# A gated long-convolution and MLP kernel with its filter transform folded twice, shift transfers on GpSimd, more norm applies on ScalarE and reordered output pairs

## The chip, the cores and the metric

The kernel runs on one core of one Trainium2 chip, in one launch. The metric is the device time of that core in microseconds, from the start of the program to its end; less is better. The arithmetic is in bf16, with sums in float32.

## The reference

The input x is 2048 rows of 640 columns. Two branches work on it and a gate mixes them.

```
g = sigmoid((x * gate_w).sum(-1))
# branch a: a causal convolution as long as the sequence
kv = (sum over 4 taps of shifted k * shift_k) * v
y  = irfft(rfft(kv padded to 4096) * rfft(ssm_k padded to 4096))[:2048] + kv * ssm_D
a  = x * y
# branch b: token shift and MLP
h  = gelu(layernorm(x) @ w1)                  # 640 -> 640
hs = the four quarters of h's columns, shifted by +1, -1, +2, -2 rows, @ w2
x1 = x + hs
b  = x1 + gelu(layernorm(x1) @ w3) @ w4       # 640 -> 1536 -> 640
out = g * a + (1 - g) * b
```

## The kernel before

The rows are 16 tiles of 128, in four blocks of 512. One SBUF arena holds everything, and its regions are used again and again by later stages.

**First norm and first layer.** `ln1` takes the mean and variance of each tile on VectorE (`bn_stats`), the power -0.5 on GpSimd, and applies both to the tile. For tiles 0 to 7 the result is transposed on TensorE and evicted by ScalarE; for tiles 8 to 15 VectorE applies the norm (`ln_apply`) and a DMA transposes it. `mm1` multiplies by w1, five groups of 128 features, with a gelu on ScalarE behind each. The fifth group holds the last 32 features of each quarter, which are to be shifted by different numbers of rows: line 924 copies four strips of 32 partitions from the gelu's buffer `hx` into `hT`, each at its own offset, on VectorE. The other four groups need no copy, since `mm2` reads them at an offset.

**Second layer and second norm.** `mm2(t)` multiplies the shifted features by w2 and adds x (on TensorE by an identity for tiles 0 to 7, in line 959 on VectorE for the rest). `ln2` takes the row sums that come with it. `ln_math` is three steps on GpSimd and, between the second and the fourth, one on VectorE: the variance, a one-column tensor_scalar. For tiles 0 to 7 VectorE applies the norm, for 8 to 15 ScalarE; a DMA transposes. `mm3` and `mm4` are the layers of the MLP, in blocks of 512 rows.

**The filter.** ssm_k is transformed once, in five chunks of 128 channels. `h_load` brings a chunk in; `h_fold` makes even and odd parts of it about its middle (`krev` is the reversed copy that ScalarE makes, `fo` the two parts, 1024 columns each), and two DMA transposes turn them into `het`. `h_chunk` multiplies them by cosine and sine tables (`Rh`, and `Zn` for two special rows), 20 matmuls of 512 columns a chunk, and ScalarE evicts the spectrum to `HF`.

**The convolution.** For two halves of 320 channels (g) and four blocks of 512 rows (b), `kv_block` forms kv and folds it, `x_fwd` transforms it, `combine` prepares the sums between blocks. `unit(hh, c)` multiplies spectra on VectorE, 2560 columns at a time. Some of its sums are made by accumulating DMAs from GpSimd's queue.

**The output.** `final(hh, c, q, k)` transforms back one pair of tiles: TensorE, an eviction on ScalarE, a sum and a difference on VectorE, a flip on TensorE, a scaled eviction on ScalarE, the product with q on VectorE. The k-th of the 16 pairs is added to the output by an accumulating DMA from GpSimd where k is below `KACC` = 12; for the last four, VectorE adds the MLP's part from `X`, and SyncE stores plainly. Where a pair accumulates, `base(t)` has stored a first value of that row's MLP branch (the scaled residual) and `mm4(t)` has accumulated its product; where it doesn't, an identity matmul in `mm4` brings the residual in.

**The order.** Each engine runs its instructions in order. The order is a list of operation numbers written out by hand, `SEQUENCE`; `schedule` walks it with a cost model that only chooses PSUM banks and a few extra dependencies. SyncE issues the plain loads and stores and all transposes, GpSimd the accumulating DMAs. Line 669 is the helper of tensor_tensor, 674 of tensor_scalar, 679 of ScalarE's activations, 689 of matmuls, 861 of the power on GpSimd, 237 of a DMA's issue and 234 of a transpose's.

Of the kernel before, what the change touches and what calls it, by code (L numbers as in the profile page):

```python
# [7 lines left out]
U16 = mybir.dt.uint16  # L8
# [4 lines left out]
class Op:  # L13
    __slots__ = ("idx", "eng", "fns", "ins", "outs", "dur", "bias", "nbytes", "preds", "succs", "rank",
                 "tp", "early", "cost", "free", "grp", "tile", "ordinal", "waits", "inc", "value", "dsem", "dval", "snap", "snapd", "start", "end", "order", "lat")

    def __init__(self, idx, eng, fns, ins, outs, dur, bias, nbytes):
        self.idx = idx
        self.eng = eng
        self.fns = fns  # L20
        self.ins = ins
        self.outs = outs
        self.dur = dur
        self.bias = bias
        self.nbytes = nbytes
        self.preds = {}
        self.succs = []
# [5 lines left out]
        self.lat = 0.0  # L33
        self.free = None
        self.tile = None
# [87 lines left out]
def regions(ap):  # L123
# [3 lines left out]
    t = ap.tensor  # L127
# [26 lines left out]
    for lo, hi in runs:  # L154
        b0, b1 = (f0 + lo) * esz, (f0 + hi) * esz
# [18 lines left out]
class Prog:  # L174
# [51 lines left out]
    def dma(self, queue, out, in_, bias=0.0, transpose=False, slow=False, free=None, early=False, accum=False, fn=None):  # L226
# [11 lines left out]
        issue = (350.0 + n / 90.0) if transpose else (970.0 if queue == "pool" else 470.0)  # L238
# [5 lines left out]
        op.cost = n * esz / 256 * 1.65 if transpose else n * esz / run * ((46 + 0.087 * run) if accum else (8 + 0.0435 * run)) / 16  # L244
# [26 lines left out]
    def schedule(self, sequence, backlog=3000.0):  # L271
# [4 lines left out]
        done = []  # L276
        avail = [0.0] * 8
# [4 lines left out]
        for i in sequence:  # L282
            o = ops[i]
            st = max([free[o.eng]] + [ops[p].end + d for p, d in delays[i]])
            if o.nbytes and not o.tp and not o.early:
                st = max(st, dfree - backlog)
            t = o.tile
# [15 lines left out]
            if o.nbytes:  # L303
                dfree = max(st + 0.5 * o.dur, dfree) + o.cost
                o.end = max(dfree, o.end) + o.lat
                if o.cost > 500 and not o.tp and not o.early:
# [122 lines left out]
def _folded_dft():  # L429
# [12 lines left out]
    p = np.arange(128)[:, None]  # L442
    no = np.stack([p, p + 128])
    ne = np.where(no == 0, 256, no)
    Rh = np.stack([np.cos(w * 2 * k * ne),
                   np.where(k == 0, no == 0, -np.sin(w * 2 * k * no)),
                   np.cos(w * (2 * ko + 1) * no),
                   -np.sin(w * (2 * ko + 1) * ne)])
    Z = np.zeros((3, 128, 128))
    Z[:2, :, 0] = ((-1.) ** ne)[:, :, 0]  # L450
    Z[2, 0] = 1.
# [6 lines left out]
    Rh = Rh.transpose(2, 0, 1, 3)  # L458
    G = G.reshape(2, 2, 2, 128, 256).transpose(3, 0, 2, 1, 4)
    return (R, np.concatenate([Rh.reshape(128, 2048), Z.transpose(1, 0, 2).reshape(128, 384)], 1),  # L460
            G.reshape(128, 8 * 256))


def bass_gated_mix__ssm_conv_h3__mixer_s_mlp__prompt_kernel(
# [33 lines left out]
    def ps(n, cls):  # L498
# [3 lines left out]
    SEQUENCE = [2, 3, 10, 11, 12, 31, 6, 57, 8, 1, 13, 14, 15, 16, 17, 18, 19, 20, 21, 22, 23, 24, 25, 7, 9, 0, 4, 28, 5, 56, 29, 63, 58, 64,  # L502
# [684 lines left out]
```

## Time and profile before

| | |
|---|---|
| Median of 3 runs | 235.55 us (234.9 to 235.9) |
| The profiled execution | 235.56 us, span 233.8 us |
| TensorE (PE) busy | 221.1 us, 95% |
| VectorE (DVE) busy | 220.1 us, 94% |
| ScalarE (ACT) busy | 170.3 us, 73% |
| GpSimd (POOL) busy | 105.9 us, 45% |
| DMA | 45.48 MB, mean 195 GB/s |

The span runs from the first to the last instruction on the core; the rest of the execution's time lies around it. Busy time is the time in which an engine has at least one instruction under way. A row of the groups names a line, an engine, an operation, its shapes and its count, then the busy time, the mean time of one, and the idle time of the engine just before such instructions, with what ended it.

### The profile page before, as it was taken

The page shows a single profiled execution, that of the slowest core. Times are in us where ns is not written, and L with a number is a line of the kernel's source. Part 1 is how long each engine was busy: PE and PEld are TensorE (multiplying, and loading weights), DVE is VectorE, ACT ScalarE, POOL GpSimd, SP SyncE. Part 2 cuts the span into 40 slices and gives each one's busy share as a digit, 9 for nine tenths or more (in the row PEclk, how much of TensorE's full clock was granted, in tenths as well). Part 3 has the DMA queues.
Part 4 walks back from the last instruction along what each step waited for, and adds up shares of the span by engine and source line. Part 5 has one row for each costly group of instructions (what it writes and reads, how often), then busy time and mean ns, then how long its engine had stood idle before and what let it go on. Part 6 is the DMA issues. An engine that isn't in the chain of part 4 may idle for free.

```text
span 233.8 us, 4171 instructions
## 1 busy us (share of the span) xinstructions
PE 221.1 (95%) x1501; PEld 134.6 (58%) x1501; DVE 220.1 (94%) x402; ACT 170.3 (73%) x317; POOL 105.9 (45%) x122
## 2 busy tenths in 40 slices
PE   7999999989998999999999999999999999999960
PEld 2598665436554656544775456654666556776630
DVE  6998999999988999998999999999989999979994
ACT  2799699488796899769949897577655387288881
POOL 0330406274495801196376693246024332456870
PEclk9999999999999999999999999999999999999997
DMA  5999959898878999978638988999978987989998
GB/s 161 360 345 250 253 146 271 246 277 204 140 181 176 240 213 317 343 212 180 157 97 145 187 189 163 146 191 206 259 142 145 196 140 142 185 98 111 95 109 165
DMA packets 63785, 45.48 MB, mean 195 GB/s; under 512 B 28818, under 2 KB 59028, under 8 KB 63764
## 3 DMA queue, kind: packets, MB, share of 16 engines
q1 hardware_dynamic: 54748, 33.33, 55.2%
q0 software_dynamic: 8832, 11.80, 34.9%
q8 instruction: 12, 0.20, 0.3%
q10 hardware_dynamic: 184, 0.08, 0.1%
q14 instruction: 9, 0.07, 0.1%
HBM read 24.22 MB, written 6.55 MB: 132 GB/s over the span
## 4 chain that ended last, share of the span: by engine, by line
PE 45%; DVE 9%; POOL 3%; ACT 2%; issue 1%
PE PSall L689 45%; DVE arena L669 8%; ACT arena L679 2%; POOL arena L674 1%; POOL arena L861 1%; POOL arena L669 1%; DVE arena L959 0%; DVE arena L674 0%
## 5 line engine op out<-in xcount | busy, mean ns | idle before, releaser
L689 PE MATMUL PSall<-arena 128*128 128x320 bf16 (+5 forms) x1444 | 213.7, 307 | 5.3 <-DVE arena L669 2.4
L669 DVE TENSOR_TENSOR arena<-arena 128x640 bf16<-128x640 bf16 (+5 forms) x247 | 182.3, 793 | 3.0 <-ACT arena L679 1.9
L689 PEld LDWEIGHTS PSall<-arena 128*128 128x128 bf16 (+1 forms) x1444 | 130.5, 98 | 86.9 <-DVE arena L669 4.2
L679 ACT ACTIVATE arena<-PSall 128x512 bf16<-128x512 f32 (+6 forms) x189 | 107.7, 634 | 29.4 <-PE PSall L689 25.2
L679 ACT ACTIVATE arena<-arena 128x640 bf16<-128x640 bf16 (+4 forms) x62 | 42.2, 703 | 6.7 <-POOL arena L669 2.7
L861 POOL TENSOR_TENSOR arena<-arena 128x1 f32<-128x1 f32 (+1 forms) x26 | 29.3, 1128 | 31.9 <-DVE arena L674 31.5
L674 POOL TENSOR_SCALAR arena<-arena 128x1 f32<-128x1 f32 (+2 forms) x41 | 24.8, 608 | 34.7 <-DVE arena L959 12.0
L237 POOL DMA_DIRECT2D out_dram<-arena x28 | 30.5, 1197 | 20.5 <-ACT arena L679 15.0
L679 ACT ACTIVATE arena<-PSall,arena 128x640 bf16<-128x640 f32 (+1 forms) x32 | 20.6, 658 | 20.0 <-PE PSall L689 19.9
L237 POOL DMA_DIRECT2D arena<-arena x12 | 14.9, 1242 | 32.1 <-DVE arena L669 28.2
L674 DVE TENSOR_SCALAR arena<-arena 128x640 bf16<-128x640 bf16 (+2 forms) x49 | 14.4, 307 | 3.4 <-POOL arena L674 1.6
L857 DVE BATCH_NORM_STATS2 arena<-arena 128x6 f32<-128x320 bf16 x32 | 14.6, 479 | 2.0 <-DMA arena<-in_A_q_dram 1.7
L669 POOL TENSOR_TENSOR arena<-arena 128x1 f32<-128x1 f32 (+1 forms) x11 | 10.3, 943 | 2.9 <-DVE arena L674 2.5
L715 PE MATMUL PSall<-arena 128*128 128x512 bf16 x15 | 5.4, 536 | 1.6 <-DVE arena L711 1.6
L959 DVE SCALAR_TENSOR_TENSOR arena<-PSall,arena 128x640 bf16<-128x640 f32 x8 | 6.4, 808 | 0.1
L924 DVE TENSOR_SCALAR arena<-arena 32x256 bf16<-32x256 bf16 (+1 forms) x24 | 5.9, 244 | 0.5
L679 ACT ACTIVATE PSall<-PSall 128x640 f32<-128x640 f32 x8 | 5.6, 699 | 0.1
L715 PEld LDWEIGHTS PSall<-arena 128*128 128x128 bf16 x15 | 1.9, 132 | 4.6 <-issue 2.5
L903 PE MATMUL PSall<-arena 128*128 128x128 bf16 x40 | 3.6, 219 | 0.3
L718 ACT ACT_TABLE_LOAD x1 | 1.3, 1283 | 2.7 <-issue 2.7
L903 PEld LDWEIGHTS PSall<-arena 128*128 128x128 bf16 x40 | 2.4, 97 | 1.4 <-DVE arena L858 0.4
L858 DVE BATCH_NORM_AGGREGATE arena<-arena 128x2 f32<-128x12 f32 x16 | 3.0, 197 | 0.0
(24 smaller groups left out, 9.6 us busy)
## 6 DMA issues: line engine op xcount, KB each, us to landing
arena<-arena POOLq DMA_DIRECT2D x12, 640.0 KB, 6.3
arena<-in_A_k_dram SPq DMA_DIRECT2D x14, 400.0 KB, 4.1
arena<-in_A_q_dram SPq DMA_DIRECT2D x14, 320.0 KB, 6.9
out_dram<-arena POOLq DMA_DIRECT2D x20, 160.0 KB, 4.2
arena<-in_A_ssm_k_dram SPq DMA_DIRECT2D x5, 512.0 KB, 4.4
arena<-in_A_v_dram SPq DMA_DIRECT2D x16, 160.0 KB, 3.9
arena<-in_B_w_dram SPq DMA_DIRECT2D x1, 1920.0 KB, 8.8
out_dram<-arena SPq DMA_DIRECT2D x10, 160.0 KB, 3.7
```

The costliest lines, as they stand in the source:

```text
L237: fn = lambda e: e.dma_start(out, in_, **kw)
L669: P.op(eng, lambda e: e.tensor_tensor(o, real(a), real(b), op), [a, b], [o], dve_ns(o, [a, b], 2) if eng == "dve" else 500)
L674: P.op(eng, lambda e: e.tensor_scalar(o, real(a), s1, s2, op0=op0, **({} if op1 is None else {"op1": op1})), [a] + aps, [o], dve_ns(o, [a] ...
L679: P.op("act", lambda e: e.activation(real(o), real(a), f, bias=bias, scale=scale, **({"accum_out": accum} if accum is not None else {})), ...
L689: fns.append(lambda e, l=l, r=r, i=i: e.matmul(real(o), l, r, start=(i == 0), stop=(i == last)))
L715: P.op("pe", lambda e: e.matmul(real(pw), warm[:, 0:128], warm[:, 128:640], start=True, stop=True), [warm], [pw], 427.0 if i < 14 else 216.0)
L857: P.op("dve", lambda e, o=o, i=i: e.bn_stats(o, i), [i], [o], 400)
L858: P.op("dve", lambda e: e.bn_aggr(bna[:, t, :], bns[k]), [bns[k]], [bna[:, t, :]], 120)
L861: P.op("pool", lambda g: g.tensor_tensor(o, a, e, ALU.pow), [a, e], [o], dur)
L903: P.op("pe", [lambda e, c=c, pb=pb, xn=xn: e.transpose(real(pb)[:, 128 * c:128 * (c + 1)], xn[:, 128 * c:128 * (c + 1)], ident) for c in r ...
L924: P.op("dve", lambda e, o=hT[q, 4, c0:c0 + n], i=hx[q, :]: e.tensor_scalar(o, i, 1.0, None, op0=ALU.mult), [hx[q, :]], [hT[q, 4, c0:c0 + n ...
L959: P.op("dve", lambda e: e.scalar_tensor_tensor(x, real(pr), 1.0, x, op0=ALU.mult, op1=ALU.add, accum_out=st[1, 0][:, t:t + 1]), [pr, x], [ ...
```

## The change

- **The filter's even bins are folded twice.** `h_fold` now takes the reversed copy in halves, and puts the element at the middle into two places, with five small steps in place of two. `h_chunk` first forms the sum and the difference of the two halves of `het` on VectorE (two operations of 1024 columns, `pq`), and repairs one partition of them (two of 512). The even bins then take one matmul where they took two; a chunk has 15 matmuls of 512 columns in place of 20. `pq` lies where the chunk's loaded filter lay, so the load of the chunk after next waits for these matmuls. The table `Rh` shrinks from 2432 to 1920 columns.
- **Shift transfers on GpSimd.** For blocks 1 to 3 the four strips are moved by DMAs from GpSimd's queue, 16 in all; block 0 keeps VectorE's copies.
- **More norm applies on ScalarE.** For tiles 8 to 15 of the first norm GpSimd computes minus mean times rstd, and ScalarE applies the norm.
- **The variance step** of the second norm goes from VectorE to GpSimd, for all 16 tiles.
- **Output pairs.** The pairs of blocks 2, 1, 0 of both halves come first (k from 0 to 11), and those of block 3 of both halves last. So tiles 12 to 15 are stored plainly, and their `base` and accumulating stores are gone; tiles 0 to 7 now have a `base` of 640 columns where it was 320.
- **The order list** is written anew for all engines. In GpSimd's queue the shift transfers stand among the steps of both norms. On VectorE the four new steps of filter chunks 0 and 1 stand between the kv products of half 0, and those of chunks 2 to 4 later, around the last products of half 0 and the first of half 1. The first output pairs stand ahead of most of half 1's spectral products.
- Some of the planner's durations differ, it now limits the descriptors in flight on SyncE, and accesses count as whole 4-byte words.

The diff, cut to its core:

```diff
@@ regions
-        b0, b1 = (f0 + lo) * esz, (f0 + hi) * esz
+        b0, b1 = (f0 + lo) * esz // 4 * 4, ((f0 + hi) * esz + 3) // 4 * 4
@@ schedule
+            while o.ring and sum(r for e, r in ring if e > st) + o.ring > 2048:
+                st = min(e for e, r in ring if e > st)
...
-    SEQUENCE = [2, 3, 10, 11, 12, 31, 6, 57, 8, 1, 13, 14, 15, 16, 17, 18, 19, 20, 21, 22, 23, 24, 25, 7, 9, 0, 4, 28, 5, 56, 29, 63, 58, 64,
...
+    hpq = [V(oXF + 10240 + 2048 * i, 2048).rearrange("p (e s b c) -> p e s b c", e=2, s=2, b=4) for i in range(2)]
@@ h_fold
-        act(kr[:, :, 1:256], k[:, :, 511:256:-1], ACTF.Copy)
-        tt(fo[:, 1], k[:, :, 0:256], kr, ALU.subtract)
-        tt(fo[:, 0], k[:, :, 0:256], kr, ALU.add)
-        ts(fo[:, 0, :, 0:1], k[:, :, 256:257], 1.0, None, ALU.mult)
+        back = bass.AP(AR, k.offset + 511, [list(k.ap)[0], [512, 4], [-256, 2], [-1, 127]])
+        act(kr[:, :, :, 1:128], back, ACTF.Copy)
+        halves = k.rearrange("p b (h n) -> p b h n", h=2)[:, :, :, 0:128]
+        f4 = fo.rearrange("p e b (h n) -> p e b h n", h=2)
+        tt(f4[:, 1], halves, kr, ALU.subtract)
+        tt(f4[:, 0], halves, kr, ALU.add)
+        tt(f4[:, 0, :, 0, 0:1], k[:, :, 128:129], k[:, :, 384:385], ALU.add)
+        tt(f4[:, 1, :, 1, 0:1], k[:, :, 128:129], k[:, :, 384:385], ALU.subtract)
+        tt(f4[:, 1, :, 1, 0:1], f4[:, 1, :, 1, 0:1], k[:, :, 0:1], ALU.add)
@@ h_chunk
+        tt(pq[:, :, 0], ev[:, :, :, 0, :], ev[:, :, :, 1, :], ALU.add)
+        tt(pq[:, :, 1], ev[:, :, :, 0, :], ev[:, :, :, 1, :], ALU.subtract)
+        for s, op in ((0, ALU.add), (1, ALU.subtract)):
+            tt(pq[0:1, 0, s], ev[0:1, 1, :, 0, :], ev[0:1, 0, :, 1, :], op)
...
-                pairs = [(Rh[:, y, kk, 128 * m:128 * (m + 1)], ev[:, eo, :, kk, :]) for kk in range(2)]
-                if y == 0:
-                    pairs.append((Zn[:, 2, :], ev[:, 1, :, 0, :]))
-                if j == 0 and r == 1:
-                    pairs += [(Zn[:, kk, :], ev[:, 0, :, kk, :]) for kk in range(2)]
+                if j < 2:
+                    pairs = [(Rhe[:, r, m, :], pq[:, r, m])]
+                else:
+                    pairs = [(Rho[:, r, kk, 128 * m:128 * (m + 1)], ev[:, 1 - r, :, kk, :]) for kk in range(2)]
+                if j == 0:
+                    pairs += [(Zn[:, 0, :], ev[:, 0, :, 0, :])] if r == 0 else [(Zn[:, 1, :], pq[:, 0, 0]), (Zn[:, 2, :], ev[:, 0, :, 0, :])]
@@ ln_math
-        ts(s[3], s[1], s[4], None, ALU.subtract)
+        tt(s[3], s[1], s[4], ALU.subtract, eng="pool")
@@ ln1
+            if t >= LN1A:
+                rstd, off = st[0, 5][:, t:t + 1], st[0, 4][:, t:t + 1]
+                ts(off, bna[:, t, 0:1], -1.0, rstd, ALU.mult, ALU.mult, eng="pool")
+                act(xn, x, ACTF.Identity, scale=rstd, bias=off)
+                P.dma(sp, xt[:, :, (t % 4) * 128:(t % 4 + 1) * 128], xn, transpose=True)
+                continue
@@ mm1
+                    if sc >= 1:
+                        P.dma("pool", hT[q, 4, c0:c0 + n], hx[q, :])
+                        continue
@@ summed, tile_rows, base, mm4
-        return 8 * hh + 2 * (3 - t // 4) < KACC
+        return t < 12
...
+        if t >= 12:
+            return
...
+        if t < 12:
+            x, o = tile_rows(t)
+            P.dma("pool", o, x, accum=True)
@@ the pairs
-    for hh in range(2):
-        for c in (3, 2, 1, 0):
-            for q in range(2):
-                at(final, hh, c, q, 8 * hh + 2 * (3 - c) + q)
+    k = 0
+    for group in ((2, 1, 0), (3,)):
+        for hh in range(2):
+            for c in group:
+                for q in range(2):
+                    at(final, hh, c, q, k)
+                    k += 1
```

More of the change, by code (lines that the diff above doesn't have):

```diff
@@ L14 @@
     __slots__ = ("idx", "eng", "fns", "ins", "outs", "dur", "bias", "nbytes", "preds", "succs", "rank",
-                 "tp", "early", "cost", "free", "grp", "tile", "ordinal", "waits", "inc", "value", "dsem", "dval", "snap", "snapd", "start", "end", "order", "lat")
+                 "tp", "early", "cost", "free", "grp", "tile", "ordinal", "waits", "inc", "value", "dsem", "dval", "snap", "snapd", "start", "end", "order", "lat", "ring")
     def __init__(self, idx, eng, fns, ins, outs, dur, bias, nbytes):
@@ L237, in dma @@
             fn = lambda e: e.dma_start(out, in_, **kw)
-        issue = (350.0 + n / 90.0) if transpose else (970.0 if queue == "pool" else 470.0)
+        issue = (1240.0 + n / 1200.0) if transpose else 970.0 if queue == "pool" else 530.0
         op = Op(len(self.ops), queue, [fn], [in_], [out], issue, bias, n * esz)
@@ L243, in dma @@
         run = esz * min(run_of(out), run_of(in_))
-        op.cost = n * esz / 256 * 1.65 if transpose else n * esz / run * ((46 + 0.087 * run) if accum else (8 + 0.0435 * run)) / 16
+        op.cost = n * esz / 256 * 1.72 if transpose else n * esz / run * ((46 + 0.087 * run) if accum else (8.4 + 0.0457 * run)) / 16
+        op.ring = 0 if queue == "pool" else n * esz // 256 if transpose else n * esz // run
+        if queue != "pool" and op.ring > 200 and not transpose:
+            op.dur = 660.0
         op.lat = 1150.0 if transpose else 3000.0 if accum else 2300.0
@@ L441, in _folded_dft @@
                         -np.sin(w * (2 * ko + 1) * n), -np.sin(w * (2 * ko + 1) * m)], 1)
[L442 to L451, printed above, removed]
+    i = np.arange(128)[:, None]
+    th, ph = w * 2 * k * i, lambda a: w * (2 * ko + 1) * a
+    cos, sin, row = np.cos(th), -np.sin(th), i == 0
+    sin[0] = np.sin(np.pi / 2 * k)[0]
+    sin[:, 0:128] *= ~row
+    b0 = np.cos(ph(128))
+    Rh = np.concatenate([cos[:, 0:128], cos[:, 128:256], sin[:, 0:128], sin[:, 128:256],
+                         np.where(row, 1 - b0, np.cos(ph(i))), np.where(row, b0, -np.cos(ph(256 - i))),
+                         -np.sin(ph(np.where(row, 128, i))), -np.sin(ph(256 - i)),
+                         np.where(row, np.cos(np.pi / 2 * k[:, 0:128]), 0.), np.zeros((128, 256))], 1)
+    Rh[:, 1664] = (-1.) ** i[:, 0]
+    Rh[0, 1792] = 1.
     m = np.arange(256, dtype=np.float64)[None, :] + .5
@@ L457, in _folded_dft @@
                   -2. * np.sin(w * (2 * ko + 1) * m)]) / 1024
-    Rh = Rh.transpose(2, 0, 1, 3)
     G = G.reshape(2, 2, 2, 128, 256).transpose(3, 0, 2, 1, 4)
-    return (R, np.concatenate([Rh.reshape(128, 2048), Z.transpose(1, 0, 2).reshape(128, 384)], 1),
-            G.reshape(128, 8 * 256))
+    return R, Rh, G.reshape(128, 8 * 256)
 def bass_gated_mix__ssm_conv_h3__mixer_s_mlp__prompt_kernel(
@@ L612, in bass_gated_mix__ssm_conv_h3__mixer_s_mlp__prompt_kernel @@
     kst = [V(oXF + 10240 + 2048 * i, 2048).rearrange("p (b n) -> p b n", b=4) for i in range(2)]
-    krev = [V(oXF + 14336 + 1024 * i, 1024).rearrange("p (b n) -> p b n", b=4) for i in range(2)]
+    krev = [V(oXF + 14336 + 1024 * i, 1024).rearrange("p (b h n) -> p b h n", b=4, h=2) for i in range(2)]
+    hpq = [V(oXF + 10240 + 2048 * i, 2048).rearrange("p (e s b c) -> p e s b c", e=2, s=2, b=4) for i in range(2)]
     het = [V(oXF + 16384 + 2048 * i, 2048).rearrange("p (e b k c) -> p e b k c", e=2, b=4, k=2) for i in range(2)]
@@ L636, in small @@
         return sm[:, o:o + n]
-    st = {(l, f): small(NT) for l, f in [(0, 3), (0, 5)] + [(1, f) for f in range(6)]}
+    st = {(l, f): small(NT) for l, f in [(0, 3), (0, 4), (0, 5)] + [(1, f) for f in range(6)]}
     gst = {f: small(NT) for f in range(6)}
@@ L985, in summed @@
     def summed(hh, t):
[L986 removed]
+        return t < 12
     def tile_rows(t):
[L989 to L990 removed]
+        return X[:, t, :], out[0, 128 * t:128 * (t + 1), :]
     def base(t):
+        if t >= 12:
+            return
         x, o = tile_rows(t)
@@ L1056, in final @@
         two = lambda a: a[:, ts_:td + 1:td - ts_, hs]
-        full, gy, ab = qb[k % 8], gyb[k % 8], (abb[k % 4] if k < 12 else abl[k - 12])
+        full, gy, ab = qb[2 * ((2 - c) % 4) + q], gyb[k % 8], (abb[k % 4] if k < 12 else abl[k - 12])
         qt = full[:, :, hs]
```

31 lines of the change are left out of this document (16 added, 15 removed), and 123 rows, old and new, of the table SEQUENCE.

## The prediction

> **What bounds the kernel now.** I read the page's busy table first, then the busy time by stage, then the groups by form, then the waits, and last the timeline of two places. The median of the runs is 235.55 us; the profiled execution took 235.56 us, of which 233.8 is its span and 1.76 lies around it. All sums below are made against that execution, so they need no correction to the median. About 0.5% (1.2 us) is what a measurement of this kernel can tell from no change.
>
> ```profile
> span 233.8 us, 4171 instructions
> PE 221.1 (95%) x1501; PEld 134.6 (58%) x1501; DVE 220.1 (94%) x402; ACT 170.3 (73%) x317; POOL 105.9 (45%) x122
> ```
>
> Two engines are nearly full, TensorE and VectorE. Which one sets the end has to be read by stage (busy us of PE, PEld, DVE, ACT, POOL in each stretch):
>
> ```profile
> 0.00:24.00 24.00, 22.00 (x245) 15.72 (x246) 20.34 (x73) 16.81 (x44) 4.85 (x13) 1.00 1.00 283
> 24.00:102.00 78.00, 75.54 (x479) 43.32 (x477) 74.86 (x165) 63.53 (x115) 35.85 (x49) 1.00 0.95 233
> 102.00:107.00 5.00, 4.74 (x23) 1.98 (x21) 4.79 (x8) 2.78 (x6) 4.72 (x5) 1.00 0.60 136
> 107.00:209.00 102.00, 102.00 (x643) 62.71 (x642) 99.02 (x105) 69.81 (x122) 46.33 (x44) 1.00 0.85 165
> 209.00:234.00 25.00, 16.86 (x119) 10.87 (x116) 21.11 (x53) 17.35 (x34) 14.19 (x13) 0.94 0.94 118
> ```
>
> From 107 to 209 us PE is full and DVE lacks 3.0 us of it; at the end PE has 8.1 us idle, while DVE runs on without a gap to 230.8. The chain of waits (start, us, what) shows the same, one long piece of PE, and after it almost only DVE:
>
> ```profile
> 106.61 102.03 PE PSall L689 x640
> 212.61 4.04 DVE arena L669 x10
> ```
>
> So DVE's own work, 220.1 us, plus its idle time, 13.7 us, is the span, and of the idle time about 3.7 us (start, before 24) and 3.7 us (after 209, mostly the landing of the last output) belong to the frame. The other 6.3 us lie between 24 and 209, and these are what a change can take away or add to. The granted clock is 1.00 in every stage up to 209 us, so it plays no part.
>
> What DVE waits for, from the groups by form (busy, mean ns, idle before):
>
> ```profile
> L669 DVE TENSOR_TENSOR arena<-arena 128x640 bf16<-128x640 bf16 x80 | 36.5, 482 | 1.7 <-ACT arena L679 1.3
> L669 DVE TENSOR_TENSOR arena<-arena 128x320 bf16<-128x320 bf16 x40 | 11.6, 320 | 0.3
> L674 DVE TENSOR_SCALAR arena<-arena 128x640 bf16<-128x640 bf16 x24 | 10.2, 433 | 0.6 <-POOL arena L861 0.5
> L669 DVE TENSOR_TENSOR arena<-arena 128x1024 bf16<-128x1024 bf16 x10 | 6.7, 680 | 0.0
> L674 DVE TENSOR_SCALAR arena<-arena 128x1 f32<-128x1 f32 x20 | 3.9, 194 | 2.8 <-POOL arena L674 1.6 <-ACT arena L679 1.2
> L924 DVE TENSOR_SCALAR arena<-arena 32x256 bf16<-32x256 bf16 x16 | 3.6, 222 | 0.3
> L924 DVE TENSOR_SCALAR arena<-arena 32x512 bf16<-32x512 bf16 x8 | 2.3, 287 | 0.2
> ```
>
> The reader is to see the fifth line: twenty one-column instructions, 3.9 us of work, have 2.8 us of waiting in front of them. Sixteen of them are the variance step of the second norm, which stands in DVE's queue between two steps on GpSimd.
>
> **VectorE's work.** The five filter chunks get 10 additions and subtractions of 1024 columns: 10 x 0.680 = 6.80 us (the same form, half the run length). They get 10 one-partition row repairs of 512 columns: between the rows of 320 (0.320) and 640 columns (0.482) that is 0.417 each, 4.17 us; ACT's 1x320 row at 456 ns beside 128x320 at 526 says that one partition saves little. The four-element repairs go from 5 to 15, at the 0.152 to 0.155 of the 128x1 and 128x4 rows: +1.50. Sum added: 12.47. Taken away: 8 shift copies of 256 columns (0.222) and 8 of 512 (0.287), 4.07; 8 first-norm applies, 8 x 0.433 = 3.46; 16 variance steps, 16 x 0.194 = 3.10. Sum removed: 10.63. Net +1.84 us. Neighbouring DVE instructions overlap by some 0.06 us (the rows add to more than the busy 220.1), which favours removing long ones over short ones; with 0.06 taken off each of the 30 added and 40 removed, the net is +2.4. I keep 1.84, and 2.4 as the upper end.
>
> **TensorE's work.** A chunk takes 15 matmuls of 512 columns in place of 20, so 25 fall away; the row has 92.4 us for 390, 0.237 each, 5.9 us. All lie in the stage 24 to 102, where PE falls from 75.5 to 69.6 of 78 us. PE did not set the end there alone, so I price this at nothing by itself; the cover is DVE, with 74.9 us in the same stage. The identity matmuls of the last stage number eight before and after.
>
> **ScalarE.** Eight norm applies more, at the 0.823 of its 128x640 row: +6.6 us in the stage to 102 (63.5 to 70.1 of 78). The base scalings go from eight of 320 and eight of 640 columns to twelve of 640, 11.0 to 9.9 us, late and beside idle time: nothing. Each apply waits for a GpSimd step and holds the gelus and evictions queued behind it.
>
> **GpSimd.** Sixteen shift transfers at 1.20 us an issue (its other DMA rows: 1.197 and 1.242) are 19.2 us; the variance step is 1.06 (its 128x1 TENSOR_TENSOR row), nine of sixteen before 102 us, 9.5 us; eight mean offsets at 0.61, 4.9 us. Four accumulating stores fewer later, -4.8. In the stage to 102 us GpSimd goes from 35.9 to about 69.5 of 78 us. Behind a shift transfer, which waits for its gelu, the norm steps queue. Landing is not seen for such a transfer: the nearest are 1.9 us (80 KB plain store) and 6.3 (640 KB accumulate); I take 3, as 16 to 32 KB is nearer to the first. In the new order some 7 us of matmuls stand between the gelu of block 512 and the first second-layer matmul that reads its shifted rows; four issues and a landing are 7.8. That costs PE under 1 us, which it has.
>
> **SyncE and the outputs.** Four base stores of 0.5 us fewer; the chunk loads now wait for the matmuls that read the new sums in the same buffer. The accumulated and plain output bytes stay the same: nothing.
>
> **The waits.** The variance step's 2.8 us go from DVE, and with them the 0.5 us of an apply at 71.16 us, behind the same tile's chain: -3.3. The final pairs begin earlier in DVE's order, ahead of most of the second half's products; of the 1.9 us that DVE waits for ACT at the final pairs and combines I take half, -0.95. New: the first of the four new steps of a chunk waits for the transposes. By the old order of wait, 2.8/20 = 0.14 each, five make 0.7 (bounds: 0, since 6.8 to 9 us of DVE work lie between the fold and these steps and two transposes issue and land in about 5.8; and 5 x 1.1, the longest such wait, 5.5). Sum: 235.56 + 1.84 - 3.3 - 0.95 + 0.7 = 233.85, so 233.9 us.
>
> **Where a rule speaks against it.** While DVE runs a string of bf16 additions, GpSimd's small steps stretch:
>
> ```profile
> 62.41 5.90 POOL L861 TENSOR_TENSOR arena<-arena 128x1 f32<-128x1 f32 x2 [2.21 <-DVE arena L674]
> 64.08 3.83 DVE L669 TENSOR_TENSOR arena<-arena 128x1280 bf16<-128x1280 bf16 x8
> ```
>
> Two powers that take 0.56 us each at the start take 5.90 here. DVE's own 128x2560 rows do not stretch (1472 ns from 30 to 66 us, 1485 from 140 to 200). GpSimd's DMA issues do not either: 1.19 to 1.20 us at 146, 153 and 170 us, with DVE full. The Trainium skill (SBUF — State Buffer, SBUF: two separate sides) says that GpSimd and a two-port VectorE instruction exclude each other for a whole instruction, and that a DMA issued by GpSimd then starves for its descriptors. On the small steps the trace agrees with that rule; on the issues it does not.
>
> **Rivals.** (1) More gain: with PE 5.9 us lighter, every wait of DVE from 24 to 209 goes: 235.56 + 1.84 - 6.3 = 231.1. For it: PE was full with DVE. Against: from 107 on PE's work is the same as before. Chance 0.20. (2) The waits half return, at the applies of the longer GpSimd chain: 233.85 + 1.65 = 235.5, no change. Chance 0.12. (3) Slower: GpSimd, in order, becomes late before 102 us. It has 8.5 us of idle left there; it waited 12.0 us for the residual sums alone (two waits). If its forced waits stay at 12.0, it is 3.5 us late and the second norm's applies on DVE wait for it: 233.85 + 3.5 = 237.4, and 240.7 if the 3.3 us gain is lost with it; between them, 239. It decides from the point at which forced waiting passes 8.5 us. For it: 69.5 of 78. Against: much of the old waiting was for the variance step itself (16.1 us in that stage). Chance 0.26. (4) Each of the 16 transfers waits half a 1.49 us DVE instruction before it can issue, 11.9 us, which lifts GpSimd to 81.4 of 78: 3.4 late, and 3.3 lost, 240.6. The issue rows above speak against it. Chance 0.04. [...] (5) ACT, at 70.1 of 78, holds PE and then DVE in the front: the 3.3 lost, 237.2. Chance 0.04.
>
> **The numbers.** The forecast has 0.34, from 232.8 to 235.2: 0.24 of it faster, 0.10 the same. Faster: 0.24 + 0.20 = 0.44. Same: 0.10 + 0.10 of case 2 = 0.20. Slower: 0.02 + 0.26 + 0.04 + 0.04 = 0.36. Cases of both signs hold most of the chance; the likeliest one's own range is 232.8 to 235.2. The range 230.3 to 239.6 takes in case 1, DVE's upper sum, and all but the ends of cases 1, 3 and 4.
>
> **What would show it.** Right: DVE busy 221.8 to 222.5, no one-column variance rows on DVE, PE near 215, the DVE idle between 24 and 209 us at 3 to 4 us. Wrong: DVE idle in front of the norm applies or the new sums with GpSimd or a transpose as releaser; GpSimd over 90% busy from 24 to 102; PE idle in front of second-layer matmuls with a GpSimd DMA as releaser; ACT's applies waiting for GpSimd with PE idle behind them.

## The result and the profile after

The changed kernel takes 256.78 us in the median (254.47 to 257.32, four runs) against 235.73 us for the kernel before (234.9 to 236.17, four runs). The ratio is 1.0879 [1.0806, 1.0952]: 21 us slower, where 1.7 us less was forecast. (A ratio leaves out executions more than 1.5% above the fastest of the same kernel; the ranges name them too.) The profiled execution took 257.32 us, of which 255.1 is its span. Its busy table:

```profile
span 255.1 us, 4160 instructions
PE 222.2 (87%) x1476; PEld 132.8 (52%) x1476; DVE 219.5 (86%) x392; ACT 175.9 (69%) x321; POOL 157.1 (62%) x158
```

VectorE (DVE) has as much work as before, 219.5 us against 220.1. It is its idle time that grew, from 13.7 to 35.6 us. So the extra time is waiting, and the busy time by stage shows where (stretch, its length, then busy us of PE, PEld, DVE, ACT, POOL, then the granted clock, the DMA share and GB/s):

```profile
24.00:102.00 78.00, 72.95 (x453) 41.19 (x451) 73.54 (x150) 67.43 (x117) 61.35 (x64) 0.96 0.93 223
...
126.00:132.00 6.00, 4.23 (x22) 1.86 (x20) 6.00 (x6) 2.93 (x6) 6.00 (x2) 1.00 0.70 139
132.00:138.00 6.00, 0.00 (x0) 0.00 (x0) 6.00 (x7) 0.00 (x0) 6.00 (x1) 0.82 0.00 0
138.00:144.00 6.00, 0.00 (x0) 0.00 (x0) 6.00 (x6) 0.00 (x0) 6.00 (x1) 0.50 0.00 0
144.00:150.00 6.00, 2.37 (x8) 1.19 (x9) 1.07 (x1) 3.93 (x6) 5.69 (x9) 0.50 0.30 50
150.00:156.00 6.00, 6.00 (x22) 2.42 (x21) 0.00 (x0) 4.10 (x9) 0.97 (x4) 0.75 1.17 157
156.00:209.00 53.00, 51.81 (x331) 31.91 (x329) 42.90 (x46) 36.15 (x65) 22.52 (x24) 1.00 0.90 170
```

From 132 to 144 us TensorE, ScalarE and the DMA engines do nothing at all, while VectorE is full and GpSimd is "busy" with one single instruction. Then it is VectorE's turn to stand still, until 157 us. The timeline of GpSimd there (start, us, engine, line, operation, operands, count, and the idle time before it with its releaser):

```profile
125.14 1.24 POOL L238 DMA_DIRECT2D arena<-arena  x1 [3.25 <-DVE arena L681]
125.93 19.19 POOL L681 TENSOR_TENSOR arena<-arena 128x1 f32<-128x1 f32 x1
145.20 0.56 POOL L882 TENSOR_TENSOR arena<-arena 128x1 f32<-128x1 f32 x1
...
148.16 1.88 POOL L238 DMA_DIRECT2D arena<-arena  x1
```

A subtraction on one column, the variance step of tile 11, takes 19.19 us; the same step takes 0.19 us at 120.26 us. (In this kernel L681 is the helper of tensor_tensor, L686 of tensor_scalar, L692 of activations, L702 of matmuls, L882 of the power, L238 of a DMA's issue.) The same stretch in the timeline of VectorE:

```profile
113.43 31.64 DVE L681 TENSOR_TENSOR arena<-arena 128x2560 bf16<-128x2560 bf16 x33
157.39 5.76 DVE L681 TENSOR_TENSOR arena<-arena 128x2560 bf16<-128x2560 bf16 x5 [12.32 <-DMA arena<-arena]
```

Of ScalarE:

```profile
146.07 0.92 ACT L692 ACTIVATE arena<-arena 128x640 bf16<-128x640 bf16 x1 [17.14 <-POOL arena L681]
```

And of TensorE:

```profile
126.39 4.09 PE L702 MATMUL PSall<-arena 128*128 128x512 bf16 x20 [0.25 <-ACT arena L692]
147.63 11.15 PE L702 MATMUL PSall<-arena 128*128 128x320 bf16 x41 [17.14 <-ACT arena L692]
```

VectorE runs 33 additions and products of bf16 without a gap from 113.43 to 145.07 us. GpSimd's step ends in the moment in which this string ends, at 145.12. Behind it in GpSimd's queue stand the power and the offset of tile 11. ScalarE's norm apply of tile 11 needs the offset and waits 17.14 us; the evictions and gelus behind that apply wait with it, and TensorE, whose banks are not emptied, waits 17.14 us for them. GpSimd's queue also holds the accumulating DMAs that make sums of the spectral products, the next one issued at 148.16: VectorE, having run through all that it could, waits 12.32 us for its landing. The chain of waits tells the same in four lines (start, us, what):

```profile
126.39 18.75 POOL arena L681
146.07 0.95 ACT arena L692 x2
147.01 10.87 DMA arena<-arena x2
...
161.34 33.49 PE PSall L702 x207
```

The clock adds to it: it is granted at 0.50 from 138 to 150 us and 0.75 to 156, and returns to 1.00 once TensorE has run again for some microseconds.

A second such step is in the trace, 14.70 us at 94.42, but VectorE lost only 2.4 us behind it. A third case, 5.73 us for two steps at 38.57, held the issue of a shift transfer, for which TensorE waited 4.22 us.

### The profile page after: what moved, and what is told of

Its sections match the earlier page's. It is cut to its first block, busy times and chain, and to the rows that moved or that the text cites. A ratio compares the mean times of both kernels' runs of the same rounds, so it can differ in the third digit from the quotient of the medians.

```text
span 255.1 us, 4160 instructions
## 1 busy us (share of the span) xinstructions
PE 222.2 (87%) x1476; PEld 132.8 (52%) x1476; DVE 219.5 (86%) x392; ACT 175.9 (69%) x321; POOL 157.1 (62%) x158
## 4 chain that ended last, share of the span: by engine, by line
DVE 38%; POOL 24%; PE 19%; DMA 6%; ACT 5%; issue 4%; SPq 2%; DVEq 0%; ACTq 0%
DVE arena L681 33%; PE PSall L702 17%; POOL arena L686 11%; POOL arena L681 8%; ACT arena L692 5%; POOL arena L882 5%; DMA arena<-arena 4%; PE PSall L728 2%; DVE arena L878 2%; DMA arena<-in_A_k_dram 2%; SPq L235 1%; SPq L238 1%; DVE arena L989 1%; DVE arena L686 1%; POOL arena L238 1%
## 5 line engine op out<-in xcount | busy, mean ns | idle before, releaser
L702 PE MATMUL PSall<-arena 128*128 128x320 bf16 (+5 forms) x1419 | 214.6, 311 | 25.4 <-ACT arena L692 19.9
L681 DVE TENSOR_TENSOR arena<-arena 128x640 bf16<-128x640 bf16 (+7 forms) x282 | 190.3, 739 | 25.5 <-DMA arena<-arena 15.3
L702 PEld LDWEIGHTS PSall<-arena 128*128 128x128 bf16 (+1 forms) x1419 | 128.5, 99 | 110.2 <-ACT arena L692 25.6
L692 ACT ACTIVATE arena<-PSall 128x512 bf16<-128x512 f32 (+6 forms) x189 | 108.7, 637 | 21.5 <-PE PSall L702 17.9
L692 ACT ACTIVATE arena<-arena 128x640 bf16<-128x640 bf16 (+2 forms) x66 | 48.9, 759 | 36.2 <-POOL arena L681 19.1
L686 POOL TENSOR_SCALAR arena<-arena 128x1 f32<-128x1 f32 (+2 forms) x49 | 54.5, 1118 | 17.6 <-DVE arena L989 7.0
L238 POOL DMA_DIRECT2D arena<-arena x28 | 24.3, 870 | 36.2 <-DVE arena L681 30.5
L681 POOL TENSOR_TENSOR arena<-arena 128x1 f32<-128x1 f32 (+1 forms) x27 | 29.1, 1084 | 15.5 <-ACT arena L692 12.6
L238 POOL DMA_DIRECT2D out_dram<-arena x24 | 26.3, 1246 | 14.7 <-DVE arena L681 8.9
L882 POOL TENSOR_TENSOR arena<-arena 128x1 f32<-128x1 f32 (+1 forms) x26 | 26.5, 1022 | 8.4 <-DVE arena L686 7.6
L692 ACT ACTIVATE arena<-PSall,arena 128x640 bf16<-128x640 f32 (+1 forms) x32 | 20.0, 655 | 13.8 <-PE PSall L702 13.7
L686 DVE TENSOR_SCALAR arena<-arena 128x640 bf16<-128x640 bf16 (+1 forms) x20 | 7.2, 370 | 2.4 <-POOL arena L882 2.4
L989 DVE SCALAR_TENSOR_TENSOR arena<-PSall,arena 128x640 bf16<-128x640 f32 x8 | 6.4, 811 | 0.0
L692 ACT ACTIVATE PSall<-PSall 128x640 f32<-128x640 f32 x8 | 5.6, 697 | 0.1
L954 DVE TENSOR_SCALAR arena<-arena 32x256 bf16<-32x256 bf16 x8 | 1.7, 218 | 0.1
```

What stands on the lines that cost most here:

```text
L238: fn = lambda e: e.dma_start(out, in_, **kw)
L681: P.op(eng, lambda e: e.tensor_tensor(o, real(a), real(b), op), [a, b], [o], dve_ns(o, [a, b], 2) if eng == "dve" else 500)
L686: P.op(eng, lambda e: e.tensor_scalar(o, real(a), s1, s2, op0=op0, **({} if op1 is None else {"op1": op1})), [a] + aps, [o], dve_ns(o, [a] ...
L692: P.op("act", lambda e: e.activation(real(o), real(a), f, bias=bias, scale=scale, **({"accum_out": accum} if accum is not None else {})), ...
L702: fns.append(lambda e, l=l, r=r, i=i: e.matmul(real(o), l, r, start=(i == 0), stop=(i == last)))
L882: P.op("pool", lambda g: g.tensor_tensor(o, a, e, ALU.pow), [a, e], [o], dur)
```

## The experiments

The first theory, S in the expectations: a GpSimd step that reads SBUF does not get in while VectorE runs two-input instructions back to back, and waits to the end of such a string. The rival was the prediction's own, load on GpSimd: too many steps and transfers in its queue.

**var_on_vector: the variance step back on VectorE.**

```diff
-        tt(s[3], s[1], s[4], ALU.subtract, eng="pool")
+        ts(s[3], s[1], s[4], None, ALU.subtract)
```

> The changed kernel with one edit: the variance step of the second norm is back on VectorE, at the same places of the order list. Theory S (starving): in the changed kernel one-column GpSimd steps of 0.2 us took 14.7 and 19.2 us while VectorE ran additions and products without a gap; ScalarE's norm apply waited 17.1 us for the second of them, and PE 17.1 us for ScalarE. A VectorE step that itself waits for GpSimd makes a gap, so the long stalls go: 235 to 242 us, GpSimd's longest step under 6 us. Theory O (overload: GpSimd has too much to do, 157 us busy): little changes, as only 16 steps of 0.2 us go: 253 to 257 us. Theory L (the new order list is bad by itself): 250 us or more.

Measured: 262.06 us (261.45 to 262.68), ratio 1.1123 [1.1086, 1.1159]. Slower still, and a miss for theory S; the number lies in the range of L, that the new order list is bad by itself, which one_wait below speaks against. The timeline of GpSimd:

```profile
127.60 4.53 POOL L882 TENSOR_TENSOR arena<-arena 128x1 f32<-128x1 f32 x1
132.21 14.82 POOL L681 TENSOR_TENSOR arena<-arena 128x1 f32<-128x1 f32 x1
```

And that of VectorE beside it:

```profile
131.74 15.24 DVE L681 TENSOR_TENSOR arena<-arena 128x2560 bf16<-128x2560 bf16 x12
```

The next step of the same tile, the offset, takes the place of the variance and lasts 14.82 us, again to the end of VectorE's string. So the stall is not tied to the variance step: here too the last step before ScalarE's apply fell into the string.

**shifts_on_vector: all shift transfers taken off GpSimd.**

```diff
-                    if sc >= 1:
+                    if sc >= 4:
```

> The changed kernel with one edit: the 16 shift transfers are VectorE copies again, at the same places of the order list. Theory S: the stall at 126 to 145 us has no shift transfer near it, so it stays; the wait of PE for a shift transfer at 44 to 49 us (4.2 us) goes, VectorE gets 4.1 us of copies: 250 to 258 us. Theory O: GpSimd loses 14 us of issues, which it was short of: 240 to 246 us.

Measured: 255.43 us (254.32 to 256.85), ratio 1.0845 [1.0795, 1.0895], so not told apart from the changed kernel. The long step stays: 19.20 us at 124.38. GpSimd's busy time falls by 17 us and nothing is gained: load is not the cause.

**one_wait: VectorE waits once for tile 11's offset.** The product that follows in VectorE's list (operation 936) is made to wait for that offset (operation 564).

```diff
+    P.ops[936].preds.setdefault(564, False)
     sched = P.schedule(SEQUENCE)
```

> The changed kernel with nothing taken away and one wait added: the first of VectorE's spectral products that the order list has behind tile 11's mean offset in the second norm (the third product of the first unit's second row of sums) waits for that GpSimd step. Theory S: VectorE's pause of 1 to 2 us lets GpSimd run; the 19.2 us step, ScalarE's 17.1 us wait and PE's go: 236 to 243 us. Theories O and L: a wait more on the busiest engine costs time: 257 to 260 us.

Measured: 238.48 us (237.34 to 240.25), ratio 1.0129 [1.0069, 1.0188]. One wait takes 18.3 of the 21 us away. The timeline of GpSimd at that place:

```profile
124.35 4.03 POOL L681 TENSOR_TENSOR arena<-arena 128x1 f32<-128x1 f32 x1
```

And that of VectorE, which the wait costs 0.99 us:

```profile
129.33 20.93 DVE L681 TENSOR_TENSOR arena<-arena 128x2560 bf16<-128x2560 bf16 x17 [0.99 <-POOL arena L681]
```

The variance step still takes 4.03 us: it ends at 128.38, when VectorE has stopped (its last product before the wait ends at 128.34). The steps behind it get in before the next product starts.

**nine_waits: nine waits.** Nine pairs in the form above: the offsets of the second norm's tiles 8 to 15, and a power of the first norm.

> The changed kernel with nine waits added and nothing taken away: a VectorE instruction waits for each of the eight mean offsets of the second norm and for the power of tiles 14 and 15 in the first norm, two VectorE instructions after the place in the order list. Theory S: every stall is cut, also those at 38 to 46 us and 94 to 111 us, each pause costs about 1 us: 234 to 242 us, near the one-wait kernel. Theories O and L: 260 us or more, as nine waits are added.

Measured: 238.32 us (238.13 to 239.09), ratio 1.0124 [1.0091, 1.0157], the same as with one. The eight further waits bring nothing that can be measured, but they do not cut every long step either: one of 5.92 us at 87.43 and one of 4.47 at 39.58 remain.

**offset_on_vector: the offset of the second norm on VectorE.**

```diff
-        tt(off, mean, rstd, ALU.mult, eng="pool")
+        tt(off, mean, rstd, ALU.mult)
```

> The changed kernel with one edit: the mean offset of the second norm for tiles 8 to 15, the last step of GpSimd's chain ahead of ScalarE's apply, is made on VectorE at the same places of the order list; the variance step stays on GpSimd. Theory S (starving), with what the kernel with the variance on VectorE taught (there the offset itself took 14.8 us, behind VectorE's step): only the last step guards the chain. VectorE now stops until the power is done, and in that gap GpSimd runs: 235 to 243 us. A rival, that any one-column step on VectorE is as good or bad as the variance step was: 255 to 262 us.

Measured: 245.44 us (245.08 to 248.31), ratio 1.0447 [1.0375, 1.0518]. VectorE's queue now stops at the offset until GpSimd's power is done, which works as the wait did: tile 11's variance takes 4.03 us. But 10 us later another tile's variance step starts inside a string and lasts 11.25 us, from 134.87 to 146.12.

**fold_once_one_wait: the wait, and the filter folded once as before.** `h_fold`, `h_chunk` and the tables are those of before, and 30 VectorE instructions leave the list; all other parts of the change stay.

> The one-wait kernel with the filter folded once, as before: 25 matmuls of 512 columns come back, VectorE's 20 new sums and repairs and 10 of the 15 small ones go, the places of all others in the order list stay. By the prediction's prices VectorE loses 12.5 us of work and PE gains 5.9. If VectorE's work sets the time of the one-wait kernel (238.5): 229 to 234 us. If PE does, which is the reason for folding twice: 240 to 245 us. If order and waits do: 236 to 240 us.

Measured: 236.12 us (235.22 to 238.6, ten runs), ratio 1.0038 [1.0005, 1.0071]. The busy table of one_wait:

```profile
PE 218.4 (93%) x1463; PEld 132.4 (56%) x1476; DVE 219.3 (93%) x392; ACT 176.5 (75%) x321; POOL 138.9 (59%) x158
```

And of this kernel:

```profile
PE 220.9 (95%) x1501; PEld 134.3 (58%) x1501; DVE 211.0 (90%) x362; ACT 176.9 (76%) x321; POOL 118.3 (51%) x158
```

The second fold puts 8.3 us on VectorE and takes 2.5 off TensorE, and costs 2.4 us of time in the medians; the two intervals, this one and that of one_wait, just touch. Without it VectorE has 8.3 us less to do, yet only 2.4 come back: here VectorE waits for TensorE instead (4.5 us in front of the sums of line 970, which is L989 in the changed kernel, and 2.0 in front of another step).

**fold_once: the filter folded once, and no wait.**

> The changed kernel with the filter folded once and no wait added. Theory S, with the thought that the double fold's extra VectorE work is what closes the gaps in which GpSimd ran: no GpSimd step over 5 us, 234 to 239 us, as with the added wait (236.1). If the stall comes from the order of GpSimd's queue and not from VectorE's load: a step of 15 to 20 us near 125 us remains, 250 to 256 us.

Measured: 235.48 us (234.4 to 238.26, eleven runs), ratio 0.9987 [0.9962, 1.0012], the time of before. There is no stall in it; GpSimd's longest step, in the timeline of the profiled execution (238.26 us):

```profile
141.53 2.88 POOL L675 TENSOR_SCALAR arena<-arena 128x1 f32<-128x1 f32 x1
```

So the other parts of the change together gain and lose nothing that can be measured, and it takes the second fold to bring the stall about. How it does so is not shown; that it shifts when VectorE's string and GpSimd's step meet is an argument only.

**variance_on_gpsimd_before: the variance step alone, in the kernel before.**

```diff
-        ts(s[3], s[1], s[4], None, ALU.subtract)
+        tt(s[3], s[1], s[4], ALU.subtract, eng="pool")
```

> The kernel before with one part of the change alone: the variance step of the second norm on GpSimd for all 16 tiles. The prediction's step: VectorE loses 3.1 us of work and 2.8 us of waits, 231 to 233 us. Theory S: VectorE's step, which waits for GpSimd, was what stopped VectorE long enough for GpSimd; without it GpSimd's steps stretch over 5 us in VectorE's long strings, and ScalarE and PE wait for them: 237 to 255 us.

Measured: 234.18 us (232.78 to 237.87, ten runs), ratio 0.9933 [0.9904, 0.9961]: faster than the kernel before by 0.7%, and the best version of this study. Both expected ranges missed it. VectorE's busy time falls by 1.8 us, to 218.3. Its waiting stays, 14.0 us against 13.7: the 2.8 us in front of the one-column steps are gone, and other waits have taken their place, among them 3.6 us for ScalarE in front of L669 (before 1.9). No GpSimd step of that kernel lasts over 2.5 us.

**variance_and_shifts_before: with the sixteen shift transfers too.** The kernel before with the edit above, the transfers of the change, accesses counted as whole words, and the list re-sorted only as far as the new waits demand.

> The kernel before with two parts of the change: the variance step on GpSimd (alone 234.2) and the 16 shift transfers on GpSimd, with accesses counted as whole 4-byte words, which moves a few operations of the order list behind those that they now depend on. By the prediction's prices VectorE loses 4.1 us more: 230 to 232.5 us if VectorE's work sets the time. Theory S: GpSimd's queue holds issues between the norm steps and runs later, and PE or ScalarE wait for it: 235 to 245 us.

Measured: 248.74 us (247.0 to 249.86), ratio 1.0543 [1.0491, 1.0595], above both expected ranges. No GpSimd step lasts over 2.1 us; TensorE waits for the transfers, in its timeline:

```profile
34.87 24.26 PE L689 MATMUL PSall<-arena 128*128 128x320 bf16 x138 [5.61 <-DMA arena<-arena]
...
86.43 28.94 PE L689 MATMUL PSall<-arena 128*128 128x320 bf16 x153 [3.01 <-DMA arena<-arena]
```

The four issues end at 31.96 us and TensorE goes on at 34.87: 2.9 us to the landing. Against the kernel with the variance step alone this is 14.6 us, of which 9.9 are TensorE's waits for these transfers (four waits; 0.2 in that kernel). The rest is not taken apart; from 24 to 102 us the granted clock is 0.91 where it was 1.00. In the order of before the copies stood directly ahead of their readers, and a transfer with its issue there is a stop of TensorE; in the changed order, with work in between, the same transfers cost TensorE 4.22 us in all.

**one_wait_block1_shift_on_vector: one wait, and the shift of block 1 on VectorE.** This aims at those 4.22 us.

```diff
-                    if sc >= 1:
+                    if sc >= 2:
```

> The one-wait kernel with the shift copies of block 1 (8 of the 16 transfers) back on VectorE. In the one-wait kernel PE waits 4.2 us at 38 to 50 us for a shift transfer that stands in GpSimd's queue behind a stretched step of 5.7 us. Theory S: that wait goes, VectorE gets 1.8 us of copies: 235 to 238 us. Rival (the transfers do not matter, the loss of the front is ScalarE's): 238.5 to 241 us.

Measured: 237.65 us (236.45 to 239.37, ten runs), ratio 1.0097 [1.0064, 1.0131]. The wait aimed at does go: TensorE waits 0.6 us for transfers where it waited 4.2. But the gain of 0.8 us over one_wait lies inside the two intervals; inconclusive.

**strings: the refusal by itself.** This kernel only copies the input and leaves out all else. VectorE runs strings of twelve instructions without a gap, and GpSimd four one-column steps beside each.

> No part of the reference but a copy of its input: a measurement of GpSimd's steps beside strings of VectorE instructions, each kind twice. In each stretch VectorE runs a string without a wait, and GpSimd begins four steps at its second instruction. Kinds: additions of 128x2560 bf16 with GpSimd one-column additions; the same with VectorE's one-input scalings; additions with GpSimd one-column scalings; additions with a one-column VectorE instruction in the middle, that waits for nothing, and then one that waits for GpSimd's fourth step; additions of 640 columns; float32 additions of 1280 columns; additions with GpSimd memsets, which read nothing; additions with GpSimd additions and DMA issues by turns. Theory S: beside two-input bf16 additions a reading GpSimd step stretches to the end of the string (about 11 x 1.4 = 15 us) or to the middle, where VectorE stops for it (about 8 us); beside one-input scalings, memsets and DMA issues under 3 us. A rival, that the stretch comes of GpSimd's own queue: all steps under 3 us everywhere.

Measured, in the timeline of GpSimd, beside 128x2560 bf16 additions and then beside scalings with one input:

```profile
17.00 5.58 POOL L490 TENSOR_TENSOR arena<-arena 128x1 f32<-128x1 f32 x4 [16.57 <-DVE arena L493]
...
33.73 2.91 POOL L490 TENSOR_TENSOR arena<-arena 128x1 f32<-128x1 f32 x4 [1.06 <-DVE arena L493]
```

Four steps take 5.58 us, 1.40 each: one per VectorE instruction. Beside additions of 640 columns they take 1.58, and four memsets, which read nothing, take 0.57 beside the same additions of 2560. Each of the 44 times that a two-input VectorE instruction ended with a step pending, the step got in; it never had to wait for the end of the string. So S, in the form that a string always shuts GpSimd out to its end, is wrong. The rival's number holds, no step over 1.5 us, but not its reason: memsets in the same queue are not stretched. What the kernel shows is rarer: a step that does not get in at boundaries at which others do.

**four_small_steps: four memsets and no wait.** If it is the pattern of starts that keeps the step out (P in the expectations), and not the lack of a wait on VectorE (W), anything that breaks the pattern will do. Behind four of VectorE's instructions in that stretch a memset of four columns is put.

```diff
+    for d in (930, 933, 938, 939):
+        P.op("dve", lambda e: e.memset(bfs[:, 192:196], 0.0), [], [bfs[:, 192:196]], 70)
+        SEQUENCE.insert(SEQUENCE.index(d) + 1, len(P.ops) - 1)
     sched = P.schedule(SEQUENCE)
```

> The changed kernel with four memsets of four columns on VectorE, of some 0.06 us each, set between the spectral products at 127 to 139 us; they wait for nothing that is open, and nothing waits for them. Theory W (GpSimd's stretched step ends only where VectorE really stops and waits): nothing changes but 0.3 us of work, 254 to 258 us, with the step of 15 to 19 us still there. Theory P (where products follow each other in a fixed rhythm, a step that did not get in once never does, and anything that shifts the rhythm ends it): the long step is cut to under 6 us, 237 to 243 us.

Measured: 239.6 us (237.84 to 240.53), ratio 1.015 [1.0082, 1.0218]. The first memset in VectorE's timeline:

```profile
128.11 0.06 DVE L1192 MEMSET arena<- 128x2 uint32 x1
```

And GpSimd's timeline there:

```profile
124.91 3.30 POOL L681 TENSOR_TENSOR arena<-arena 128x1 f32<-128x1 f32 x1
128.28 1.05 POOL L882 TENSOR_TENSOR arena<-arena 128x1 f32<-128x1 f32 x1
```

The step gets in at the first memset, at 128.2, after 3.30 us. Four instructions of 0.06 us, without any wait, take 17 us off the kernel. Both this run and one_wait show that the stall is the step kept out, and not the data flow around it. How the memsets help stays open. The time lies in P's range, but P in its plain form is not borne out: in the strings run the products followed each other in a fixed rhythm of 1.402 us, and every step got in. And this run differs ahead of the first memset already: there one VectorE instruction starts 83 to 86 ns before the last one's end, where in the changed kernel it was 78 to 80.

## Why the prediction was wrong, point by point

**Where the 21 us are.** 256.8 to 238.5: the kept-out step, 18.3 us, shown by one_wait and again by four_small_steps. 238.5 to 236.1: the second fold's own price, 2.4 us, shown by fold_once_one_wait. 236.1 to 235.5: nothing that can be measured.

**VectorE's work (+1.84, at most +2.4).** Wrong in sign, by 2.4 to 2.6 us: 219.5 us in the changed kernel and 219.3 in one_wait, against 220.1. The rows of the groups by form came out as priced (busy, mean ns of one, idle before):

```profile
L681 DVE TENSOR_TENSOR arena<-arena 128x1024 bf16<-128x1024 bf16 x20 | 13.4, 677 | 3.1 <-ACT arena L692 3.1
L681 DVE TENSOR_TENSOR arena<-arena 1x512 bf16<-1x512 bf16 x10 | 4.0, 406 | 0.0
L681 DVE TENSOR_TENSOR arena<-arena 128x4 bf16<-128x4 bf16 x15 | 2.4, 169 | 0.0
L686 DVE TENSOR_SCALAR arena<-arena 128x1 f32<-128x1 f32 x4 | 0.6, 138 | 0.0
```

Ten more of 1024 columns, 6.7; the row repairs 0.406 each where 0.417 was taken; the small repairs 1.6 more. But the fold's 30 instructions, 12.3 us by their rows, add 8.3 us to the busy time: in these traces an instruction overlaps with either neighbour by some 0.07 to 0.09 us, and of a short one little is left. The allowance of 0.06 for each was too small here, 0.13 by this pair of kernels. The sixteen variance steps show the same: 3.3 us less by their row (3.9 to 0.6), 1.8 less of busy time in variance_on_gpsimd_before.

**TensorE's work.** Forecast 215 us, 5.9 less; one_wait has 218.4, 2.5 less than with one fold. Of the difference some 2.4 us (1.1% of 220) can be the clock, 0.981 on average in one_wait and 0.992 in fold_once_one_wait, which is an estimate. Pricing it at nothing was too low for the new order: with one fold VectorE waits 6.7 us for TensorE, with two for nothing of note, which is why 8.3 us of work cost only 2.4 of time. It did not pay for the work.

**The variance waits (-3.3) and the work (-3.1).** Half wrong. By itself the step is worth 1.0 us in the medians and 1.5 us in the span, not 5.9 (2.8 of waits and 3.1 of work): 1.8 of work, and the removed waits return elsewhere. Rival 2 had this half return.

**The new sums (+0.7).** The sum of wait was placed at the transposes; the rows of the new sums show no wait for one. What VectorE waits for is one fold of 1024 columns, 3.1 us, in the row above: the reversed copy comes late, since ScalarE stands behind a norm apply at that place, and the apply waits for GpSimd. In one_wait:

```profile
50.38 2.67 ACT L692 ACTIVATE arena<-arena 128x640 bf16<-128x640 bf16 x3 [3.33 <-POOL arena L686]
```

Ahead of that, GpSimd's two steps at 39.63, 5.72 us together, are the same stretching at a smaller size. With block 1's shift on VectorE the apply waits 0.22 us and this wait is gone. The size is still inside the bounds of 0 to 5.5; its cause is another.

**The final pairs (-0.95).** Not gained as far as can be seen, and not tried alone: in one_wait VectorE waits 6.0 us for ScalarE, 3.1 of it at that fold; the other 2.9 stand against 1.9 before.

**GpSimd's load and ScalarE's.** Forecast 69.5 us of 78 before 102 us, measured 61.35; ScalarE 67.43 where 70.1 was forecast; that rival 5 had a part is not seen. The issues were mis-sized: sixteen transfers take 0.55 us each to issue, not 1.20. The landing of 3 us was right for the 16 KB transfers (2.8, the median in the changed kernel) and low for those of 32 KB (4.3). "Under 1 us" for TensorE was not right: 4.22.

**The step that failed** is the price of GpSimd's small steps. The prediction took the moved variance step at the mean of its row, 1.06 us each, in a sum of GpSimd's work up to 102 us, and gave nothing to a single step that is kept out; the two stretched powers, 5.90 us, stood in it as a remark without a term. The mean was no bound: one step of 24 took 19.19 us. Rival 3 came nearest, at chance 0.26: GpSimd late and the second norm's applies behind it. But it put the wait before 102 us and on VectorE's applies, priced it at 3.5 to 7 us and made it depend on GpSimd's load. It came at 126 us, on ScalarE's applies with TensorE idle behind them (the last sign that the prediction lists), cost 18.3, and did not hang on load: GpSimd had 4.7 us of idle time in the 19 us ahead of it. It takes the second fold to bring the stall about (fold_once without it, 235.48 us), and the prediction priced the fold by VectorE's work alone.

**The rule.** The Trainium skill (SBUF — State Buffer, SBUF: two separate sides) has a VectorE instruction with two SBUF inputs and a GpSimd step that reads SBUF exclude each other for one whole instruction. The strings run agrees, at 1.40 us a step. In the kernel the step was kept out over 15 boundaries of instructions in succession at 126 us, and over 22 at 94 us (a few of those instructions had one input), which an exclusion by the instruction alone does not give. That a DMA issued by GpSimd starves, the same section states for VectorE's two-port modes and not for two inputs. The issues that the prediction held against it ran beside additions and products with two inputs, so they neither agree nor disagree with it, and no run here shows such starving: shift transfers took 0.55 us each to issue, and most accumulating ones of 640 KB 1.2 to 1.3, beside a nearly full VectorE. Rival 4 was rightly small.

**The range.** 230.3 to 239.6 held the variants in which no GpSimd step lasts over 6 us (234.2 to 239.6), save the one with the transfers in an order not made for them. It had no case for a single step that waits out a string, though the trace of before showed the stretching that such a case grows from.

## What to carry to other kernels

Before a short step is moved to GpSimd, look at what VectorE runs at the time and at who stands behind the step: its cost can be not its mean but the whole string of two-input VectorE instructions that it meets, and all that waits in order behind it. Where such a step feeds an in-order engine, let one VectorE instruction near it wait for its result; here 0.99 us of waiting bought 18.3 us. Four small instructions between the products did as well, in one run, for a reason that stays open. Price a queue of short steps by its worst row as well as by its mean, and weigh a part of a change by itself: the one-line move of the variance step was worth more than the whole.

## What the runs showed of the hardware that was not expected

- **A one-column GpSimd step can be kept out over many VectorE instructions.** Over all traces, counted where one TENSOR_TENSOR of VectorE follows another while a GpSimd step that reads is pending (it counts as let in when it ends before the second instruction does): where the second started 69 to 72 ns before the first one's end, 16 of 286 got in; at 84 ns, 85 of 124. But at 78 to 80 ns, where the step of 19.19 us was refused 15 times, it was 44 of 90. What decides stays open.
- **VectorE pays nothing for it.** Its 128x2560 instructions took 1481 ns on average in the changed kernel, with GpSimd waiting beside many of them, and 1485 before.
- **The string need not have a gap to let the step in.** With a memset of 0.06 us between two products the step got in, though the starts of the products were 1.411 us apart across it and 1.402 without; that the memset itself did it is not shown.
- **The granted clock falls to 0.50 after TensorE has stood still**: from 138 to 150 us after the stop at 130.5, and around 50 us after the stop of 4.22 us.
